# Expert 0's output for the last batch as seven products in token pairs, and earlier fetches of expert 1's weights

## The chip, the cores and the metric

The kernel runs on one core of one Trainium2 chip. The metric is the device time of one execution in microseconds (us); lower is better. Times called "at 115.84" are microseconds from the start of the profiled execution's span. The engines are called as the profile calls them: PE (TensorE; PEld is its weight load), DVE (VectorE), ACT (ScalarE), POOL (GpSimd) and SP (SyncE, here only a queue of transfers).

## What is computed

An attention over sorted blocks gives `x` (3072 tokens, 512 features); a mixture of eight experts, all of which see every token, is summed with routing weights `P`:

```python
# attention: 4 batches, 8 heads, 768 positions, 64 features; blocks sorted by a doubly normalised 8x8 matrix
x = attn_out.transpose(0, 2, 1, 3).reshape(3072, 512)
logits = x @ w_gate                       # 3072 x 8
P = np.exp(logits - logits.max())
for _ in range(8):                        # the routing's rounds
    P /= P.sum(1, keepdims=True) + 1e-09
    P /= P.sum(0, keepdims=True) + 1e-09
    P *= N / E
for e in range(E):                        # w1[e]: 512 x 1024, w2[e]: 1024 x 512
    h = np.maximum(x @ w1[e], 0.0)
    out += P[:, e:e + 1] * (h @ w2[e])
```

## The kernel before

**Stages.** Batch 0's attention comes first. Then the attention of batches 1 to 3 is woven with expert 0's work on batches 0 and 1 (`first_two`). From about 114.5 on, with the attention's buffers given back, expert 0 works on batches 2 and 3 (`last_two`, called `tail0` in the loop) while the routing's rounds run (`balance`, called `chain`). Behind that come experts 1 to 7, whose products all go by a seven-product scheme (Winograd's form of Strassen's: seven products of half size in place of eight, for sums and differences made beforehand).

**Expert 0.** `hidden0` makes `relu(x @ w1)` for 384 tokens: eight blocks `fb` of four 128x384 matmuls, each taken out of PSUM by ACT; one `next()` of it is one block. `output0` makes `h @ w2` for three tiles of 128 tokens: eight 128x512 matmuls each, and one `next()` is four of them. Batch 2's outputs are copied to `osbl` by ACT (`keep`); batch 3's are scaled with the routing weight `glog[:, t, 0]` on the way (`keep_scaled`). Copied tiles are scaled later, in SBUF, by ACT (`scale0`, 18 tiles).

**Experts 1 to 7.** `hidden(e, p, i, hT)` is one of four units for a third `p` of the tokens (1024): seven steps of two 128x512 matmuls, three ACT copies, one ACT relu and four DVE operations. `output7` is seven steps of four 128x256 matmuls for a pair of token tiles. `gather` adds a scaled product to `osbl` on DVE. Their operands are sums: `sum_w` (of w1), `sum_w2` (of w2) and `sum_h` (of the hidden layer) on POOL, `sum_x` (of x, line 139) on DVE. `sums(n)` issues the next n operations from the queue of POOL's sums.

**The rounds.** `balance` is a chain of small DVE operations (lines 446 to 475) on `glog`, 128x24x8, with small PE matmuls between them that sum over the partitions (lines 449, 454, 471). Each `yield` of it ends a piece; the loop of 56 steps says behind which step of `tail0` a piece goes. PE executes in the order in which the pinned matmuls are written, so a round's matmul that waits for DVE holds up what is written behind it. The pieces with matmuls stand behind steps 2, 4, and 8, 13, 17, 22, 26, 31, 35, 39. From step 28 on, one step of the first unit series of expert 1 (`first`, 28 steps) is written behind each step of `tail0`.

**Orders and queues.** `pin` puts an instruction behind whatever was written before it for its engine. Other instructions may be moved ahead by the scheduler that lays out each engine's stream before the run; `sum_x` on DVE, `scale0` on ACT and `balance`'s DVE operations are not pinned. Weights come by transfers issued on POOL (`load_w1`, line 81; `load_w2`, line 86), which share one queue with the loads of q, k and v (`load_batch`, line 72) and with half of the small transfers of sorted values (`vsb`, line 170; the other half goes by SP). Expert 1's w1 is fetched during batch 3's attention, w2 behind `sum_w(1)`. POOL's `sums(8)` stands at step 40 behind a one-operation gate (line 652) that reads `glog`, so that it starts when the rounds are over.

Of the kernel before, what the change touches and what calls it, by code (L numbers as in the profile page):

```python
# [13 lines left out]
F32 = mybir.dt.float32  # L14
BF16 = mybir.dt.bfloat16
AF = mybir.ActivationFunctionType
# [9 lines left out]
def kernel(  # L26
# [52 lines left out]
    def load_w1(e):  # L79
        w1t[e] = wp.tile([128, 4, F], BF16, name="w1e")  # L80
        pin(nc.gpsimd.dma_start(out=w1t[e],
                                in_=moe_w1[e].rearrange("(kk k) f -> k kk f", k=128)))

    def load_w2(e):
        w2t[e] = (wq if e else wcp).tile([128, 8, Dm], BF16, name="w2e")
        pin(nc.gpsimd.dma_start(out=w2t[e],
                                in_=moe_w2[e].rearrange("(fb k) f -> k fb f", k=128)))
# [222 lines left out]
    def output0(c0, hTs, obank, done):  # L310
        for tt in range(3):
            oacc = obank()
            for fb in range(8):
                pin(nc.tensor.matmul(oacc, hTs[:, fb, tt * 128:(tt + 1) * 128],
                                     w2t[0][:, fb, :], start=(fb == 0), stop=(fb == 7)))
                if fb == 3:
                    yield
            done(c0 // 128 + tt, oacc)
            yield

    def keep(t, oacc):
        (nc.vector.tensor_copy if t < 12 else nc.scalar.copy)(osbl[:, t, :], oacc)

    def keep_scaled(t, oacc):
        nc.scalar.activation(out=osbl[:, t, :], in_=oacc, func=AF.Copy,
                             scale=glog[:, t, 0:1])

    wct = {}

# [110 lines left out]
    def balance():  # L440
        onesc = mpc.tile([128, 128], F32)
        nc.vector.memset(onesc, 1.0)
        I128 = mpc.tile([128, 128], F32)
        nc.vector.tensor_copy(I128, Ibig)
        gm = mpc.tile([128, 1], F32)
        nc.vector.reduce_max(out=gm, in_=glog.rearrange("p t e -> p (t e)"), axis=AX.X)
        yield
        gmps = bank()[:, 0:128]
        pin(nc.tensor.matmul(gmps[0:1, :], gm, I128, start=True, stop=True))
        gm1 = mpc.tile([1, 1], F32)  # L450
        nc.vector.reduce_max(out=gm1, in_=gmps[0:1, :], axis=AX.X, negate=True)
        yield
        gnps = bank()[:, 0:128]
        pin(nc.tensor.matmul(gnps[:, 0:1], onesc[0:1, :], gm1, start=True, stop=True))
        gneg = mpc.tile([128, 1], F32)
        nc.vector.tensor_copy(gneg, gnps[:, 0:1])
        nc.scalar.activation(out=glog, in_=glog, func=AF.Exp, bias=gneg)

        rs2 = mpc.tile([128, NT], F32)
        cs2 = mpc.tile([128, E], F32)  # L460
        cs1 = mpc.tile([128, E], F32)
        yield
        for it in range(8):
            nc.vector.reduce_sum(out=rs2, in_=glog, axis=AX.X)
            nc.vector.tensor_scalar_add(rs2, rs2, 1e-9)
            nc.vector.reciprocal(out=rs2, in_=rs2)
            nc.vector.tensor_mul(glog, glog, mkap(rs2, [rs2.ap[0], rs2.ap[1], [0, E]]))
            nc.vector.reduce_sum(out=cs2, in_=glog.rearrange("p t e -> p e t"), axis=AX.X)
            yield
            csps = bank()[:, 0:128]  # L470
            pin(nc.tensor.matmul(csps[:, 0:E], onesc, cs2, start=True, stop=True))
# [3 lines left out]
            nc.vector.tensor_mul(glog, glog, mkap(cs1, [cs1.ap[0], [0, NT], cs1.ap[1]]))  # L475
            yield
# [141 lines left out]
    def sums(n):  # L618
        while n and queue:
            if next(queue[0], 0) is None:  # L620
                n -= 1
            else:
                queue.pop(0)

    def last_two():
        for bb, done in ((2, keep), (3, keep_scaled)):
            hT = htp.tile([128, 8, 1024], BF16, name="hT")
            halves = [(bb * S + c, hT[:, :, c:c + 384]) for c in (0, 384)]
            for c0, hTs in halves:
                yield from hidden0(c0, hTs, bank)  # L630
            for c0, hTs in halves:
                yield from output0(c0, hTs, lambda: op.tile([128, Dm], F32, name="oacc"), done)

    tail0, chain = last_two(), balance()
    x1, x2 = sum_x(1), sum_x(2)
    works = {0: x0, 10: x1, 14: x1, 19: x1, 23: x1, 41: x2, 43: x2, 46: x2, 48: x2}
    first = None
    for n in range(56):
        next(tail0)
        if n == 28:  # L640
            hT = htp.tile([128, 8, 1024], BF16, name="hT")
            first = units(1, 0, hT, pin)
        if first:
            next(first)
            if n == 28 + 21:
                sum_h(0, hT, 0, 3)
        if n in works:
            next(works[n], 0)
        if n in (0, 2, 4, 6, 8, 11, 13, 15, 17, 20, 22, 24, 26, 29, 31, 33, 35, 37, 39):
            next(chain)  # L650
        if n == 40:
            pin(nc.gpsimd.tensor_copy(held, glog[0:96, NT - 1, 0:2]))
            sums(8)

    hTs = {0: hT}

# [60 lines left out]
```

## Time and profile before

| What | Value |
|---|---|
| Time of three runs, median (lowest to highest) | 679.98 us (679.85 to 680.33) |
| The profiled execution: its own time; its span | 680.18 us; 678.2 us |
| Mean granted TensorE clock | 0.992 of full speed |
| Busy shares of the span: PE, DVE, POOL, ACT | 96%, 80%, 70%, 44% |
| Stage with `tail0`: start; first matmul of `output7` | 114.55; 172.51 |
| Rounds: first matmul (line 449); last `glog` update (line 475) | 116.59; 152.99 to 153.35 |
| `load_w1(1)` issued; `sum_w(1)`; `load_w2(1)` issued | 95.33; 104.14 to 113.25; 113.25 |

The span is what the profile shows of the engines; the execution's own time holds 1.98 us more around it. Busy shares are averages over stages with different limits.

### The profile page before, as it was taken

What the parts mean: (1) busy time and instruction counts of PE and PEld (TensorE: products, weight loads), DVE (VectorE), ACT (ScalarE), POOL (GpSimd) and SP (SyncE); (2) the same over time, 40 slices, a digit from 0 to 9 for tenths busy, and PEclk for the clock granted to TensorE, in tenths of its full rate; (3) what the DMA queues carried; (4) which work ended last, traced back from release to release, by engine and by line L of the source; (5) the groups of instructions that cost most, each with busy time, mean ns of one, the idle gap of its engine ahead of it and who ended that gap; (6) DMA issues with size and microseconds to landing.
All of it is one profiled execution on the core that took longest, in us unless ns stands there. A gap on an engine that the chain in (4) does not pass through costs nothing.

```text
span 678.2 us, 13166 instructions
## 1 busy us (share of the span) xinstructions
PE 651.5 (96%) x5033; PEld 436.5 (64%) x5108; DVE 545.2 (80%) x1154; ACT 298.5 (44%) x550; POOL 472.6 (70%) x499
## 2 busy tenths in 40 slices
PE   2999999999999999999999999999999999999996
PEld 1756766554566666666666666666666666666675
DVE  6727768763788888888988889888888889888896
ACT  3747764469533433334333343434333343333430
POOL 4542335007888988898997898689886999646745
PEclk9789999999999999999999999999999999999999
DMA  9898973100240330030303040034003120001223
GB/s 146 164 218 127 150 125 46 31 1 12 52 61 3 63 60 5 1 63 4 61 1 47 17 63 1 1 63 63 1 2 63 19 45 0 1 1 64 94 78 141
DMA packets 31903, 36.57 MB, mean 54 GB/s; under 512 B 2016, under 2 KB 24288, under 8 KB 31840
## 3 DMA queue, kind: packets, MB, share of 16 engines
q0 software_dynamic: 26400, 27.82, 25.9%
q1 hardware_dynamic: 5440, 7.90, 3.6%
q8 instruction: 40, 0.66, 0.4%
q14 instruction: 23, 0.19, 0.1%
HBM read 52.45 MB, written 6.29 MB: 87 GB/s over the span
## 4 chain that ended last, share of the span: by engine, by line
PE 72%; DVE 1%; issue 1%; POOL 1%; ACT 0%; DVEq 0%
PE oacc L574 37%; PE bk L487 34%; PE bk L574 1%; DVE osbl L539 1%; POOL hs L557 1%; DVE hT L523 0%; DVE hT L526 0%; ACT p L507 0%; DVEq L539 0%
## 5 line engine op out<-in xcount | busy, mean ns | idle before, releaser
L539 DVE SCALAR_TENSOR_TENSOR osbl<-oacc,glog,osbl 128x256 f32<-128x256 f32 (+1 forms) x490 | 255.7, 522 | 61.4 <-PE oacc L574 61.3
L557 POOL TENSOR_TENSOR hs<-hT 128x512 bf16<-128x512 bf16 (+2 forms) x105 | 99.5, 961 | 67.7 <-DVE hT L526 67.6
L487 PE MATMUL bk<-xtT,w1e 128*128 128x512 bf16 x475 | 143.5, 379 | 0.9
L574 PEld LDWEIGHTS <-hT 128*128 128x128 bf16 x1008 | 98.6, 98 | 64.5 <-issue 1.2
L574 PEld LDWEIGHTS <-hs 128*128 128x128 bf16 x1008 | 98.5, 98 | 64.5 <-POOL hs L557 1.5
L574 PE MATMUL oacc<-w2e,hT 128*128 128x256 bf16 x796 | 119.6, 273 | 1.0 <-ACT hT L529 0.5
L529 ACT ACTIVATE hT<-bk 128x512 bf16<-128x512 f32 x84 | 50.3, 599 | 158.2 <-PE bk L487 140.4
L557 POOL TENSOR_TENSOR hs<-hT,hs 128x512 bf16<-128x512 bf16 (+2 forms) x105 | 99.9, 959 | 4.9
L557 POOL TENSOR_TENSOR hs<-hs,hT 128x512 bf16<-128x512 bf16 (+2 forms) x105 | 100.0, 960 | 4.2 <-ACT hT L529 0.4
L487 PE MATMUL bk<-xc,wc 128*128 128x512 bf16 x319 | 96.3, 379 | 0.6 <-ACT p L507 0.2
L574 PE MATMUL oacc<-w2e,hs 128*128 128x256 bf16 x612 | 92.0, 273 | 1.6 <-POOL hs L557 0.9
L515 ACT COPY u<-bk 128x512 f32<-128x512 f32 x84 | 49.3, 587 | 95.4 <-PE bk L487 82.4
L487 PEld LDWEIGHTS <-w1e 128*128 128x128 bf16 x672 | 65.8, 98 | 10.4
L523 DVE CUSTOM_DVE_ANT_0 hT<-bk,p 128x512 bf16<-128x512 f32 x84 | 58.1, 692 | 11.5 <-ACT p L520 6.4
L533 DVE SCALAR_TENSOR_TENSOR h<-bk,hT 128x512 bf16<-128x512 f32 x84 | 57.2, 681 | 5.8 <-ACT hT L529 5.8
L520 ACT COPY p<-bk 128x512 f32<-128x512 f32 x84 | 49.4, 588 | 23.2 <-PE bk L487 23.2
L507 ACT COPY p<-bk 128x512 f32<-128x512 f32 x84 | 49.4, 588 | 20.3 <-PE bk L487 20.3
L511 DVE CUSTOM_DVE_ANT_0 hT<-bk,p 128x512 bf16<-128x512 f32 x84 | 57.3, 682 | 0.9 <-ACT hT L307 0.5
L526 DVE CUSTOM_DVE_ANT_0 hT<-bk,u 128x512 bf16<-128x512 f32 x84 | 57.2, 680 | 1.0 <-PE bk L487 1.0
L574 PE MATMUL oacc<-w2s,hs 128*128 128x256 bf16 x364 | 54.8, 273 | 0.3
L487 PEld LDWEIGHTS <-wc 128*128 128x128 bf16 x504 | 49.3, 98 | 8.0 <-issue 0.4
L487 PE MATMUL bk<-xc,w1e 128*128 128x512 bf16 x159 | 48.0, 379 | 0.0
(116 smaller groups left out, 834.9 us busy)
## 6 DMA issues: line engine op xcount, KB each, us to landing
w1e<-in_moe_w_dram POOLq DMA_DIRECT2D x8, 1024.0 KB, 8.2
w2e<-in_moe_w_dram POOLq DMA_DIRECT2D x8, 1024.0 KB, 8.9
out_dram<-osbl SPq DMA_DIRECT2D x23, 256.0 KB, 2.0
kvq<-in_v_dram POOLq DMA_DIRECT2D x3, 768.0 KB, 10.4
vsb<-vs SPq DMA_DIRECT2D x16, 97.5 KB, 4.3
vsb<-vs POOLq DMA_DIRECT2D x16, 97.5 KB, 3.9
kvq<-in_q_dram POOLq DMA_DIRECT2D x4, 384.0 KB, 12.9
kvq<-in_k_dram POOLq DMA_DIRECT2D x4, 384.0 KB, 13.5
```

Source lines behind the costliest of these rows:

```text
L487: hold(nc.tensor.matmul(ps, wa[:, kk, :], xa[:, kk, :], start=(first and kk == 0), stop=(kk == 1), skip_group_check=True))
L507: nc.scalar.copy(p1, u)
L511: nc.vector._custom_dve(TENSOR_ADD_SAT, out=c11, in0=w, in1=p1, s0=TOP, s1=0.0)
L515: nc.scalar.copy(u2, u)
L520: nc.scalar.copy(p5, v)
L523: nc.vector._custom_dve(TENSOR_ADD_SAT, out=c22, in0=u, in1=p5, s0=TOP, s1=0.0)
L526: nc.vector._custom_dve(TENSOR_ADD_SAT, out=c12, in0=v, in1=u2, s0=TOP, s1=0.0)
L529: nc.scalar.activation(out=c21, in_=u, func=AF.Relu)
L533: nc.vector.scalar_tensor_tensor(out=h3[e, p][:, i, :], in0=u, scalar=0.0, in1=c22, op0=ALU.max, op1=ALU.subtract)
L539: nc.vector.scalar_tensor_tensor(out=o, in0=ps, scalar=glog[:, t, e:e + 1], in1=o, op0=ALU.mult, op1=ALU.add)
L557: nc.gpsimd.tensor_tensor(out=c, in0=a, in1=b, op=o)
L574: nc.tensor.matmul(ps, h[:, fb, :], w[:, fb, :], start=(first and fb == 0), stop=(fb == 3), skip_group_check=True)
```

## The change

Three things. The 48 matmuls 128x512 of batch 3's outputs become, in three pairs of token tiles (18 and 21, 19 and 22, 20 and 23), 3 x 7 steps of four 128x256 matmuls; their w2 sums (`sum_w2_0`, eight POOL operations) and hidden sums (`sum_h0`, sixteen POOL operations, eight of them half as long) are new, and the outputs are taken out by four ACT operations and two DVE operations for each pair instead of two ACT operations. `load_w1(1)` moves from batch 3's attention to batch 2's. POOL's gate is gone: `sum_w2_0` and four operations of `sum_w2(1)` are written ahead of the loop, the other four at step 5 of `first`. The rounds all stand in the 44 steps ahead of the pairs (matmuls behind steps 2, 4, and 9, 15, 19, 23, 27, 33, 38, 43), and the 21 pair steps are written, three for every four, into the 28 steps of `first`. `w2s[0]` takes the first of the two buffers in which `load_w2(1)` was.

```diff
-    def hidden0(c0, hTs, hbank):
-        for fb in range(8):
+    def hidden0(c0, hTs, hbank, each=lambda n: None):
+        for n, fb in enumerate((0, 4, 1, 5, 2, 6, 3, 7)):
...
             nc.scalar.activation(out=hTs[:, fb, 0:384], in_=hps[:, 0:384], func=AF.Relu)
+            each(n)
             yield
...
                 load_batch(bb + 1, [(x, 0, 8) for x in "vkq"])
                 build_r(bb + 1, nc.gpsimd, 4)
+                if bb == 2:
+                    load_w1(1)
             else:
-                load_w1(1)
                 sums = sum_w(1)
...
-    load_w2(1)
...
+    hs0 = {}
+
+    w2s[0] = wq.tile([128, 4, 4, Dm // 2], BF16, name="w2e")
+    load_w2(1)
+
+    def sum_w2_0():
+        for k in (0, 2):
+            b11, b12 = (w2t[0][:, 4 + k:6 + k, d:d + 256] for d in (0, 256))
+            b21, b22 = (w2t[0][:, k:k + 2, d:d + 256] for d in (0, 256))
+            t1, t2, t3, t4 = (w2s[0][:, j, k:k + 2, :] for j in range(4))
+            for a, b, c in ((b12, b11, t1), (b22, t1, t2), (b22, b12, t3), (b21, t2, t4)):
+                pin(nc.gpsimd.tensor_tensor(out=c, in0=a, in1=b, op=ALU.subtract))
+
+    def sum_h0(i, hA, hB, f0=0, f1=4):
+        if f0 == 0:
+            hs0[i] = hsp.tile([128, 3, 4, 128], BF16, name="hs")
+        cs = slice(128 * i, 128 * i + 128)
+        s1, s2, s4 = (hs0[i][:, j, f0:f1] for j in range(3))
+        a11, a12 = hA[:, 4 + f0:4 + f1, cs], hA[:, f0:f1, cs]
+        a21, a22 = hB[:, 4 + f0:4 + f1, cs], hB[:, f0:f1, cs]
+        for a, b, o, c in ((a21, a22, ALU.add, s1), (s1, a11, ALU.subtract, s2),
+                           (a11, a21, ALU.subtract, a21), (a12, s2, ALU.subtract, s4)):
+            pin(nc.gpsimd.tensor_tensor(out=c, in0=a, in1=b, op=o))
+
+    def pair0(i, hA, hB):
+        a, b = 18 + i, 21 + i
...
+        def add(ps, h, w, first):
+            for fb in range(4):
+                pin(nc.tensor.matmul(ps, h[:, fb, :], w[:, fb, :], start=(first and fb == 0),
+                                     stop=(fb == 3), skip_group_check=True))
+
+        def put(t, c, ps):
+            nc.scalar.activation(out=osbl[:, t, c:c + 256], in_=ps, func=AF.Copy,
+                                 scale=glog[:, t, 0:1])
+
+        u, x = (op.tile([128, Dm], F32, name="oacc") for _ in range(2))
+        u, x0, x1 = u[:, 0:256], x[:, 0:256], x[:, 256:512]
+        add(u, hA[:, 4:8, cs], b11, True)
+        put(a, 0, u)
+        yield
+        add(x0, hA[:, 0:4, cs], b21, True)
+        yield
+        add(x1, s1, t1, True)
+        put(b, 256, x1)
+        yield
+        add(u, s2, t2, False)
+        put(a, 256, u)
+        yield
+        add(x1, s4, b22, False)
+        gather(0, a, 0, x)
+        yield
+        add(u, s3, t3, False)
+        gather(0, b, 256, u)
+        yield
+        add(u, hB[:, 0:4, cs], t4, False)
+        put(b, 0, u)
+        yield
+
+    def pairs0(hA, hB):
+        p = [pair0(i, hA, hB) for i in range(3)]
+        for i in (0, 0, 0, 0, 0, 1, 0, 1, 0, 1, 1, 1, 2, 1, 2, 1, 2, 2, 2, 2, 2):
+            next(p[i])
+            yield
+
     def last_two():
...
+        def each(n):
+            if n in (3, 7):
+                sum_h0(0, hA, hB, (n - 3) // 2, (n + 1) // 2)
+
+        yield from hidden0(3 * S, hA, bank)
+        yield from hidden0(3 * S + 384, hB, bank, each)
+        for i in (1, 2):
+            sum_h0(i, hA, hB)
+        yield from pairs0(hA, hB)
+
+    sum_w2_0()
+    sums(4)
     tail0, chain = last_two(), balance()
     x1, x2 = sum_x(1), sum_x(2)
-    works = {0: x0, 10: x1, 14: x1, 19: x1, 23: x1, 41: x2, 43: x2, 46: x2, 48: x2}
-    first = None
-    for n in range(56):
+    works = {0: x0, 11: x1, 17: x1, 21: x1, 25: x1, 47: x2, 51: x2, 55: x2, 59: x2}
+    rounds = (0, 2, 4, 6, 9, 10, 15, 16, 19, 20, 23, 24, 27, 28, 33, 34, 38, 39, 43)
+    for n in range(44):
         next(tail0)
-        if n == 28:
-            hT = htp.tile([128, 8, 1024], BF16, name="hT")
-            first = units(1, 0, hT, pin)
-        if first:
-            next(first)
-            if n == 28 + 21:
-                sum_h(0, hT, 0, 3)
...
-        if n in (0, 2, 4, 6, 8, 11, 13, 15, 17, 20, 22, 24, 26, 29, 31, 33, 35, 37, 39):
+        if n in rounds:
             next(chain)
-        if n == 40:
-            pin(nc.gpsimd.tensor_copy(held, glog[0:96, NT - 1, 0:2]))
-            sums(8)
+    hT = htp.tile([128, 8, 1024], BF16, name="hT")
+    first, n = units(1, 0, hT, pin), 0
+    for m in range(28):
+        next(first)
+        if m == 5:
+            sums(4)
+        if m == 20:
+            sum_h(0, hT, 0, 3)
+        while n * 28 < (m + 1) * 21:
+            next(tail0)
+            n += 1
...
```

More of the change, by code (lines that the diff above doesn't have):

```diff
@@ L322, in keep @@
         (nc.vector.tensor_copy if t < 12 else nc.scalar.copy)(osbl[:, t, :], oacc)
-    def keep_scaled(t, oacc):
-        nc.scalar.activation(out=osbl[:, t, :], in_=oacc, func=AF.Copy,
-                             scale=glog[:, t, 0:1])
     wct = {}
@@ L623, in sums @@
                 queue.pop(0)
-    def last_two():
-        for bb, done in ((2, keep), (3, keep_scaled)):
-            hT = htp.tile([128, 8, 1024], BF16, name="hT")
[L628 to L632, printed above, removed]
+    hs0 = {}
+    w2s[0] = wq.tile([128, 4, 4, Dm // 2], BF16, name="w2e")
@@ new lines, in pair0 @@
+    def pair0(i, hA, hB):
+        a, b = 18 + i, 21 + i
+        cs = slice(128 * i, 128 * i + 128)
+        s1, s2, s4 = (hs0[i][:, j] for j in range(3))
+        t1, t2, t3, t4 = (w2s[0][:, j] for j in range(4))
+        s3 = hB[:, 4:8, cs]
+        b11, b21, b22 = w2t[0][:, 4:8, 0:256], w2t[0][:, 0:4, 0:256], w2t[0][:, 0:4, 256:512]
+        def add(ps, h, w, first):
[27 more added lines that the diff above has]
+        yield
@@ new lines, in pairs0 @@
+    def pairs0(hA, hB):
[3 more added lines that the diff above has]
+            yield
+    def last_two():
+        obank = lambda: op.tile([128, Dm], F32, name="oacc")
+        hT = htp.tile([128, 8, 1024], BF16, name="hT")
+        for c in (0, 384):
+            yield from hidden0(2 * S + c, hT[:, :, c:c + 384], bank)
+        for c in (0, 384):
+            yield from output0(2 * S + c, hT[:, :, c:c + 384], obank, keep)
+        hT = htp.tile([128, 8, 1024], BF16, name="hT")
+        hA, hB = hT[:, :, 0:384], hT[:, :, 384:768]
+        def each(n):
[6 more added lines that the diff above has]
+        yield from pairs0(hA, hB)
@@ L634 @@
+    sum_w2_0()
+    sums(4)
     tail0, chain = last_two(), balance()
     x1, x2 = sum_x(1), sum_x(2)
-    works = {0: x0, 10: x1, 14: x1, 19: x1, 23: x1, 41: x2, 43: x2, 46: x2, 48: x2}
-    first = None
-    for n in range(56):
+    works = {0: x0, 11: x1, 17: x1, 21: x1, 25: x1, 47: x2, 51: x2, 55: x2, 59: x2}
+    rounds = (0, 2, 4, 6, 9, 10, 15, 16, 19, 20, 23, 24, 27, 28, 33, 34, 38, 39, 43)
+    for n in range(44):
         next(tail0)
-        if n == 28:
-            hT = htp.tile([128, 8, 1024], BF16, name="hT")
-            first = units(1, 0, hT, pin)
-        if first:
-            next(first)
-            if n == 28 + 21:
-                sum_h(0, hT, 0, 3)
@@ L647 @@
         if n in works:
             next(works[n], 0)
-        if n in (0, 2, 4, 6, 8, 11, 13, 15, 17, 20, 22, 24, 26, 29, 31, 33, 35, 37, 39):
+        if n in rounds:
             next(chain)
-        if n == 40:
-            pin(nc.gpsimd.tensor_copy(held, glog[0:96, NT - 1, 0:2]))
-            sums(8)
+    hT = htp.tile([128, 8, 1024], BF16, name="hT")
+    first, n = units(1, 0, hT, pin), 0
[8 more added lines that the diff above has]
+            n += 1
+            if 44 + n in works:
+                next(works[44 + n], 0)
```

## The prediction, made before the changed kernel ran

> **What bounds the kernel now.** I read the page first, then the timelines of PE, DVE, POOL and ACT from 95 to 185, then the table of stages, then single transfers.
>
> ```profile
> PE 651.5 (96%) x5033; PEld 436.5 (64%) x5108; DVE 545.2 (80%) x1154; ACT 298.5 (44%) x550; POOL 472.6 (70%) x499
> ...
> PE 72%; DVE 1%; issue 1%; POOL 1%; ACT 0%; DVEq 0%
> ```
>
> PE's matmuls are the path. In the table of stages every 40 us from 220 to 660 hold about 39.74 us of PE, so what PE gains or loses before 175 moves the end by as much. PE's losses there stand in the timeline of all engines at the start of the rounds:
>
> ```profile
> 115.84 1.28 DVE L139 TENSOR_TENSOR xc<-xtT 128x1024 bf16<-128x1024 bf16 x2
> ...
> 117.04 1.28 DVE L139 TENSOR_TENSOR xc<-xtT,xc 128x1024 bf16<-128x1024 bf16 x2
> ...
> 118.24 0.27 DVE L451 TENSOR_REDUCE gm<-bk 1x1 f32<-1x128 f32 x1
> ...
> 118.44 1.27 DVE L139 TENSOR_TENSOR xc<-xtT,xc 128x1024 bf16<-128x1024 bf16 x2
> ...
> 118.66 0.35 PE L454 MATMUL bk<-gm,onesc 1*128 1x1 f32 x2 [0.28 <-DVE gm L451]
> ...
> 119.64 0.14 DVE L456 COPY gneg<-bk 128x1 f32<-128x1 f32 x1
> ...
> 122.19 0.39 PE L471 MATMUL bk<-cs,onesc 128*128 128x8 f32 x2 [0.47 <-DVE cs L468]
> ```
>
> The scheduler has put six subtractions of `sum_x` (0.60 us start to start) into the first links of the rounds' chain: L451 and L456 leave DVE only behind them. By starts PE loses 0.45 us at L454 (eight hidden matmuls from 116.91 end their pitch of 0.1625 at 118.21), 0.65 at the first L471 (sixteen from 118.94: 121.54) and 0.44 at the third (eight 128x512 at 0.2158 from 127.11: 128.84; it starts at 129.28). POOL does nothing meanwhile:
>
> ```profile
> 113.25 0.94 POOL L86 DMA_DIRECT2D w2e<-in_moe_w_dram  x1
> 153.42 0.18 POOL L652 CAST held<-glog 96x2 bf16<-96x2 f32 x1 [39.24 <-DVE glog L475]
> ```
>
> At the seam to `output7` PE loses 1.03 us more (five groups reach 175.28 in place of 174.25), behind an ACT that is busy 19.10 of 19.10 us from 153.4 to 172.5.
>
> **The change part by part.** *The products.* 48 matmuls 128x512 at 0.2158 (twenty in 4.48 us, the last lasting 0.38) are 10.36 us; 84 of 128x256 at 0.1085 (a group of four and the next start 0.434 apart) are 9.11. Sum: −1.25 us, all of it on PE.
>
> *The rounds' places.* The least round from one L471 to the next is 3.05 us (133.81 until L468 ends at 136.79, and its start). A hidden step is 0.65 (138.40 to 139.04), an output step 0.863. The first L471 stands one hidden step later: the 0.65 goes. The next gaps are six hidden steps (3.9 us), four output steps (3.45, three times), six, five and five hidden steps (3.25 at least): all above 3.05. Only the third L471 may wait, by 0.1, because one subtraction (0.68) that must wait for batch 2's hidden steps falls into its round, as at 127.10. So 1.54 becomes 0.55: −1.0 us. The 0.45 at L454 stays.
>
> *POOL's new work ahead of the rounds.* Here a resource meets DVE that it did not meet before. The rows that show the meeting are the timeline at 61 and at 155, against a free one:
>
> ```profile
> 61.72 2.06 POOL L188 COPY qr<-kvq 128x768 bf16<-128x768 bf16 x2 [11.33 <-DMA kvq<-in_q_dram]
> 61.79 1.30 DVE L139 TENSOR_TENSOR xc<-xtT 128x1024 bf16<-128x1024 bf16 x1
> ...
> 85.60 0.68 DVE L139 TENSOR_TENSOR xtT<-xtT 128x1024 bf16<-128x1024 bf16 x1
> ...
> 155.61 0.89 DVE L139 TENSOR_TENSOR xtT<-xtT 128x1024 bf16<-128x1024 bf16 x1
> 155.91 1.61 POOL L437 TENSOR_TENSOR w2s<-w2e 128x512 bf16<-128x512 bf16 x1
> ```
>
> An L139 that starts inside a POOL operation takes 1.30 or 0.89 in place of 0.68, as long as that operation still lasts, and POOL's next operation waits for it in turn (1.61 for 1.15). The Trainium skill, SBUF — State Buffer, "SBUF: two separate sides", says it as a rule: the port pair that VectorE and GpSimd share is an exclusive lock for a whole instruction, taken by a VectorE operation with two SBUF inputs, and the other engine blocks fully; it speaks against POOL work at this place. By that rule the copy at L444 (SBUF to SBUF, one source, in a two-port mode) would wait as well, which no row here shows, and the sum would be some 0.3 us higher, an estimate.
>
> When is POOL busy? q of batch 3 lands at 74.4 + 14.3 = 88.7. w1 stands behind it in the queue and takes 5.8 more (w1 of expert 0 lands at 34.0, the w2 behind it at 39.8): 94.5. POOL's copies of batch 3 end at 95.4. `sum_w(1)` takes 9.1 (104.1 to 113.25): 104.5; the issue of w2 0.94: 105.5; `sum_w2_0` eight at 1.14: 114.6; w2 has landed by 104.5 + 9.0. `sums(4)`: 114.6 to 119.2 without a wait. The subtractions want 115.84 to 119.7. If the engines take turns, the four ahead of L451 run 116.9 to 117.5, behind POOL's next 118.65 to 119.25, 120.4 to 121.0, and 121.6: L451 is 3.4 us late, and L454, behind which PE's whole queue stands, with it. If DVE keeps the port once it has it, L451 is 1.1 late, L451 then lets POOL in, and L456 is 2.0 late. With POOL one microsecond later (a slower w1) it is 4.0; with the subtractions elsewhere it is 0. No row shows two DVE operations in a row against POOL. I take 3.4, since in both rows POOL's next operation comes right behind the DVE one. +3.4 us.
>
> *The pairs.* Each pair frees its accumulators by four `put`s and two gathers. A put is 0.4 to 0.55 us (a 512 copy 0.588, a 384 relu 0.490, scaling adds 0.13). `x1` must be free two pair steps after its put: 2.17 us (1.73 in the second pair), of which the group itself takes 0.60. ACT started 0.35 to 1.0 us behind PE in the saturated stretch, so some puts come 0 to 0.4 late. The last gather (0.48) has only 0.43 us of other matmuls in front of the step that waits for it: 0.3 to 1.0. Queued behind such a wait are PE's steps of `first`. Bounds 0 to 2.0; I take +0.6. A gain is excluded, since PE did not wait inside the old outputs (their groups follow at 1.30 us from 156.11 on). DVE's gathers (0.75 + 0.48, three times) lie beside 21 us in which it has some 4 us idle.
>
> *Hidden sums.* Sixteen POOL operations, 8 x 1.153 + 8 x 0.67 (between 0.43 for 128 and 0.92 for 384 columns) = 14.6 us, from the last hidden steps on. s1 of pair 1 is wanted about 9 us behind the last hidden step and is ready after 4.4; of pair 2, 16 against 9. Hidden; without that cover each operation late would cost 1.15. Their meeting with the last rounds' two-input operations (0.36) costs 0 to 0.5; I take 0.
>
> *w1 fetched sooner.* It needs no buffer back and 0.81 us of an idle POOL. But batch 3's sorted values (four on POOL's queue, issued 90.8 to 92.9; four on SP's) now meet it. Beside bulk loads, POOL's landed 0.3 to 1.7 us behind the last load and SP's took 6.7 in place of 3.3: 96 to 98.4 here, and they are wanted at 99.40. 0 to 1.0; I take +0.1.
>
> *The seam.* ACT still has 18 scales at 0.64, so I leave its 1.03.
>
> Sum: −1.25 − 1.0 + 3.4 + 0.6 + 0.1 = +1.85 on the profiled 680.18 (span 678.2 and 1.98 around it): 682.0. The median is 0.20 below the profiled run: 681.8.
>
> **Rivals.** *No meeting (faster).* The subtractions stand behind L451 and L456, or POOL is done before 115.8. Then the 3.4 goes: −1.55, 678.4 (677.7 to 680.0). For it: the scheduler lays the streams out anew. Against: by my clock POOL would have to be 3.4 us earlier, and the subtractions' data and buffers come free at the same moment as before. It decides as soon as POOL's last sum ends before 116.
>
> *Half a meeting (no change).* DVE keeps the port: 2.0 in place of 3.4, with pairs nearly free: 680.0 (679 to 681.3).
>
> *ACT becomes the bound (slower still).* From the last hidden step PE needs 28 x 0.433 + 21 x 0.434 = 21.2 us; ACT 16 x 0.48 + 12 x 0.5 + 18 x 0.64 = 25.2 if all scales are pulled in there. Before, the same count gave 22 for 19.1 us and PE lost 1.03, because scales are only put where the plan sees ACT idle. If the excess of 4 us lands on the puts, pairs cost 2.0 to 2.5 and the total is 683.5.
>
> *The fetch does not come sooner* because w1 holds up q instead of following it: then `queries` of batch 3 wait up to 5 us. Queue order in the rows speaks against it; it sits inside the slow cases.
>
> **How the numbers follow.** Forecast 0.36, no meeting 0.36, half a meeting 0.14, ACT-bound or fetch 0.14. About 0.2% (1.36 us) is what a measurement can tell. Faster by more: three quarters of the no-meeting case, 0.27. Slower by more: three quarters of the forecast (681.4 is near its lower half), the last case and little else, 0.43. The rest 0.30. Range: −2.25 with nothing lost gives 677.7; −2.25 + 4.0 + 2.0 + 0.1 gives 683.9. The forecast's own range is 680.4 to 683.9.
>
> **What would show it.** Right: L139 at about 117 to 123 with 1.2 to 1.8 us each and L437-like sums of 1.7 between them; PE idle 3 to 4 us before L454; L471 without waits later; 84 matmuls 128x256 into `oacc` at 0.1085 by 170. Wrong: L139 at 0.68 with POOL quiet, L454 at about 118.6; or PE idle inside the pairs of over 2 us; or a gap at 99 before the sorted values.

## The result, and the profile after

The changed kernel takes 683.64 us (median of six runs, 682.63 to 684.01) against 679.81 us for the kernel before (six runs, 679.26 to 680.33): ratio 1.0047, 95% interval 1.0037 to 1.0057. It is slower by 3.8 us; the forecast was 681.8, slower by 1.9. The profiled execution took 683.79 us, with a span of 682.0 and a mean granted clock of 0.986 (before: 680.18, 678.2 and 0.992).

Line numbers moved with the change. Before → after: the copy to `I` L444 → L440, the rounds' first reduction L451 → L447, the matmuls L449, L454, L471 → L445, L450, L467, POOL's sums of w2 L437 → L433, hidden matmuls of experts 1 to 7 L487 → L483, `output7` L574 → L570. The page's first line and the engine shares of its chain, after:

```profile
PE 653.2 (96%) x5069; PEld 440.8 (65%) x5144; DVE 543.8 (80%) x1160; ACT 299.6 (44%) x556; POOL 496.6 (73%) x522
...
PE 70%; DVE 2%; POOL 1%; ACT 1%; issue 1%; POOLq 0%; ACTq 0%; DVEq 0%
```

POOL has 24 us more work (472.6 before), and PE's share of the chain has gone from 72% to 70%, DVE's from 1% to 2%. Where, the timeline of all engines at the start of the rounds shows (start, duration, engine, line, operation; in brackets the idle time before it and who ended it):

```profile
114.01 1.16 POOL L433 TENSOR_TENSOR w2s<-w2e 128x512 bf16<-128x512 bf16 x1
114.94 0.30 DVE L440 CAST I<-Ibig 128x128 f32<-128x128 bf16 x1
...
115.43 3.08 DVE L139 TENSOR_TENSOR xc<-xtT 128x1024 bf16<-128x1024 bf16 x2
...
116.34 1.47 PE L305 MATMUL bk<-xtT,w1e 128*128 128x384 bf16 x8
116.35 1.60 POOL L433 TENSOR_TENSOR w2s<-w2e 128x512 bf16<-128x512 bf16 x1
...
117.92 1.60 POOL L433 TENSOR_TENSOR w2s<-w2e,w2s 128x512 bf16<-128x512 bf16 x1
118.43 2.24 DVE L139 TENSOR_TENSOR xc<-xtT,xc 128x1024 bf16<-128x1024 bf16 x2
120.59 0.27 DVE L447 TENSOR_REDUCE gm<-bk 1x1 f32<-1x128 f32 x1
...
121.00 0.55 PE L450 MATMUL bk<-gm,onesc 1*128 1x1 f32 x2 [3.19 <-DVE gm L447]
...
121.49 6.07 PE L305 MATMUL bk<-xtT,w1e 128*128 128x384 bf16 x20
...
127.40 0.28 PE L467 MATMUL bk<-cs,onesc 128*128 128x8 f32 x2
```

Two things stand here. First, the meeting: two L139 take 3.08 and 2.24 us where they took 1.28, POOL's sums between them 1.60 instead of 1.16, and L450 waits 3.19 us (0.28 before). Second, one that the prediction does not have: the twenty hidden matmuls behind L450 need 5.91 us from their first start to L467, where 20 x 0.1625 = 3.25. The table of windows (length; busy time and instructions of PE, PEld, DVE, ACT, POOL; then the granted TensorE clock, the DMA share, GB/s) says why:

```profile
118.40:120.20 1.80, 0.00 (x0) 0.00 (x0) 1.80 (x3) 0.00 (x0) 1.11 (x1) 0.97 0.00 0
120.20:121.00 0.80, 0.00 (x0) 0.03 (x1) 0.80 (x3) 0.00 (x0) 0.00 (x0) 0.50 0.00 0
121.00:124.00 3.00, 3.00 (x10) 1.66 (x11) 2.34 (x8) 0.95 (x2) 0.00 (x0) 0.50 0.00 0
124.00:126.80 2.80, 2.80 (x10) 1.36 (x9) 0.47 (x1) 0.98 (x2) 0.00 (x0) 0.50 0.03 6
126.80:130.00 3.20, 3.20 (x22) 1.99 (x21) 2.04 (x8) 2.28 (x5) 0.00 (x0) 0.98 0.00 0
```

While PE stood, its granted clock fell to half, and it stayed there until 126.9. The wait cost its own length, and then as much again.

Behind that, no L467 waits. The pairs (from 153.15 to the first `output7` group at 177.22) have PE wait again. PE's timeline there, the waits, and ACT's around the first:

```profile
156.85 0.59 PE L483 MATMUL bk<-xtT,w1e 128*128 128x512 bf16 x2 [0.50 <-ACT u L511]
161.23 0.59 PE L483 MATMUL bk<-xc,wc 128*128 128x512 bf16 x2 [0.32 <-ACT p L503]
```

```profile
154.63 0.47 ACT L659 ACTIVATE osbl<-oacc,glog 128x256 f32<-128x256 f32 x1 [0.26 <-PE bk L483]
155.00 1.32 ACT L605 ACTIVATE osbl<-osbl,glog 128x512 f32<-128x512 f32 x2
156.23 0.57 ACT L511 COPY u<-bk 128x512 f32<-128x512 f32 x1
```

Two scalings (L605, from `scale0`) have been laid in front of the copy L511 that frees a PSUM bank for PE. By starts, the pairs' groups come 1.96 us late in all: 0.67 and 0.49 at these two places, 0.11 to 0.25 at five more.

### The profile page after: what moved, and what is told of

The parts are those of the page before. It is cut to its first block, busy times and chain, and to the rows that moved or that the text cites. A ratio compares the mean times of both kernels' runs of the same rounds, so it can differ in the third digit from the quotient of the medians.

```text
span 682.0 us, 13286 instructions
## 1 busy us (share of the span) xinstructions
PE 653.2 (96%) x5069; PEld 440.8 (65%) x5144; DVE 543.8 (80%) x1160; ACT 299.6 (44%) x556; POOL 496.6 (73%) x522
## 4 chain that ended last, share of the span: by engine, by line
PE 70%; DVE 2%; POOL 1%; ACT 1%; issue 1%; POOLq 0%; ACTq 0%; DVEq 0%
PE oacc L570 35%; PE bk L483 34%; POOL hs L553 1%; DVE osbl L535 1%; PE oacc L655 1%; DVE h L529 1%; ACT hT L525 1%; DVE hT L519 0%; ACT osbl L605 0%; PE bk L570 0%; POOLq L794 0%; ACT u L511 0%; DVE hT L522 0%; ACT osbl L659 0%; ACT p L516 0%
## 5 line engine op out<-in xcount | busy, mean ns | idle before, releaser
L535 DVE SCALAR_TENSOR_TENSOR osbl<-oacc,glog,osbl 128x256 f32<-128x256 f32 (+1 forms) x496 | 251.9, 522 | 63.8 <-PE oacc L570 62.0
L483 PE MATMUL bk<-xtT,w1e 128*128 128x512 bf16 x475 | 155.0, 378 | 1.6 <-ACT u L511 0.5
L553 POOL TENSOR_TENSOR hs<-hT 128x512 bf16<-128x512 bf16 (+2 forms) x105 | 99.9, 961 | 62.4 <-DVE hT L522 62.3
L570 PEld LDWEIGHTS <-hT 128*128 128x128 bf16 x1008 | 98.6, 98 | 63.8 <-issue 1.2
L570 PEld LDWEIGHTS <-hs 128*128 128x128 bf16 x1008 | 98.0, 97 | 56.4 <-issue 0.8
L570 PE MATMUL oacc<-w2e,hT 128*128 128x256 bf16 x796 | 119.7, 273 | 0.4
L553 POOL TENSOR_TENSOR hs<-hs,hT 128x512 bf16<-128x512 bf16 (+2 forms) x105 | 100.2, 963 | 4.7
L553 POOL TENSOR_TENSOR hs<-hT,hs 128x512 bf16<-128x512 bf16 (+2 forms) x105 | 100.0, 961 | 4.9
L483 PE MATMUL bk<-xc,wc 128*128 128x512 bf16 x318 | 96.0, 379 | 0.8 <-ACT p L503 0.3
L570 PE MATMUL oacc<-w2e,hs 128*128 128x256 bf16 x612 | 91.7, 272 | 0.7
L511 ACT COPY u<-bk 128x512 f32<-128x512 f32 x84 | 49.4, 588 | 95.4 <-PE bk L483 85.8
L483 PEld LDWEIGHTS <-w1e 128*128 128x128 bf16 x672 | 65.8, 98 | 18.5 <-issue 1.6
L570 PE MATMUL oacc<-w2s,hs 128*128 128x256 bf16 x364 | 54.5, 272 | 0.3
L483 PEld LDWEIGHTS <-wc 128*128 128x128 bf16 x504 | 49.3, 98 | 7.0 <-issue 0.7
L483 PE MATMUL bk<-xc,w1e 128*128 128x512 bf16 x159 | 48.0, 379 | 0.1
```

What stands on the lines that cost most here:

```text
L483: hold(nc.tensor.matmul(ps, wa[:, kk, :], xa[:, kk, :], start=(first and kk == 0), stop=(kk == 1), skip_group_check=True))
L511: nc.scalar.copy(u2, u)
L553: nc.gpsimd.tensor_tensor(out=c, in0=a, in1=b, op=o)
L570: nc.tensor.matmul(ps, h[:, fb, :], w[:, fb, :], start=(first and fb == 0), stop=(fb == 3), skip_group_check=True)
```

## The account

Each row is one profiled execution, in us from the span's start, and differences. "Start" is the first matmul of the rounds (L445, before L449); "stand" is from there to L450, with 8 x 0.1625 of matmuls and some 0.4 of its own in it; "next" from L450 to the first L467 (one hidden step, 0.65, shorter in the kernels with the old places of the rounds); "total" from the start to the last group of matmuls of the kernel. The kernels below the first two are the experiments that follow.

| Kernel | Start | Stand | Next | Total |
|---|---|---|---|---|
| before | 116.59 | 2.07 | 3.53 (0.47 of it wait) | 557.41 |
| after | 116.03 | 4.97 | 6.40 | 561.84 |
| after, subtractions held (a_sumx) | 116.84 | 1.71 | 3.57 | 555.21 |
| after, 18 fillers (a_fill) | 116.85 | 4.96 | 3.62 | 559.12 |
| after, scalings held (a_scale) | 116.61 | 4.96 | 5.22 | 560.11 |
| after, four sums later (a_sums_gate) | 117.73 | 2.07 | 3.62 | 557.52 |
| a_sumx without the products (a_noprod) | 116.88 | 1.71 | 3.94 | 556.54 |
| both held (a_both) | 116.84 | 1.72 | 3.57 | 555.02 |
| before, subtractions held (b_sumx) | 116.40 | 1.71 | 3.07 | 556.10 |

The starts differ between executions by what comes early in them: the first L192 is already at 70.46 before and at 69.89 after, the same 0.57 apart, and over all traces here it lies between 69.82 and 71.85. From one fixed matmul of batch 3's attention (L192 near 98.4) to the start, before, after and the first held kernel need the same: 98.42 to 116.59, 97.86 to 116.03 and 98.67 to 116.84 are 18.17 each. So the earlier fetch of w1 shows no cost and no gain at PE.

After against before the total is +4.43: the stand +2.90; the half clock 6.40 − 3.57 = +2.83; the products −1.25, worked out and not measured here; the waits of the first and third round gone, −1.09; the pairs +1.96; the seam to `output7` −0.62 (its third group starts 2.15 behind the first, 2.77 before); the last output's wait for POOL's L553 0.88 to 0.2, −0.7. Sum +4.03; 0.4 are not placed.

## The experiments

The theory: POOL's sums and VectorE's subtractions share something that only one of them holds at a time; the subtractions, laid into the first link of the rounds by the scheduler, are stretched; PE stands; the stand brings the clock down. The rivals: VectorE's order alone, without POOL; ACT in the pairs; products that cost as much as they save.

**The subtractions held in their written place.** `sum_x(1)` and `sum_x(2)` then stand behind the rounds' pieces, and POOL's sums meet none of them.

```diff
 def sum_x(p):
...
-            nc.vector.tensor_tensor(out=c, in0=a, in1=b, op=ALU.subtract)
+            (pin if p else lambda ins: ins)(nc.vector.tensor_tensor(out=c, in0=a, in1=b, op=ALU.subtract))
```

> The changed kernel, with sum_x(1) and sum_x(2) kept in the written order on DVE, so that their six first subtractions stand at steps 11, 17, 21 of the rounds and later, when POOL is idle, and not ahead of the chain's links at L447 and L452. PE, ACT and POOL streams are the same as in the changed kernel. Theory 1 (the subtractions meet POOL's last four w2 sums, PE stands for 3.4 us at L450, and its clock then halves for 20 matmuls, 2.7 us): both go, L450 starts at about 117.7, the 20 matmuls behind it take 3.3 us, the subtractions last 0.68 us, and the kernel takes 677.6 us (677.0 to 678.6). Rival A (PE waits there for something else, the sums' memory traffic or the order of the rounds): 683.6, unchanged. Rival B (the clock drop is set by the clock's own window and not by the wait): about 3 us gained, 680.5.

Measured: 678.09 us (677.57 to 679.08), ratio to before 0.9964, interval 0.9950 to 0.9977, inside the range written: 5.5 us faster than the change, and faster than the kernel before. The timeline of all engines at the same place:

```profile
116.04 1.15 POOL L433 TENSOR_TENSOR w2s<-w2e,w2s 128x512 bf16<-128x512 bf16 x1
...
117.14 1.15 POOL L433 TENSOR_TENSOR w2s<-w2e 128x512 bf16<-128x512 bf16 x1
117.25 0.28 DVE L447 TENSOR_REDUCE gm<-bk 1x1 f32<-1x128 f32 x1 [0.95 <-PE bk L445]
118.26 1.15 POOL L433 TENSOR_TENSOR w2s<-w2e,w2s 128x512 bf16<-128x512 bf16 x1
118.55 0.29 PEld L450 LDWEIGHTS bk<-gm,onesc 1*128 1x128 f32 x2 [0.32 <-ACT hT L307]
118.55 0.38 PE L450 MATMUL bk<-gm,onesc 1*128 1x1 f32 x2
```

POOL's sums last 1.15 each, the reduction waits for PE rather than PE for it, and the clock is 1.00 from 114 on. Stand and half clock are both gone.

**Fillers in the stand.** Is the half clock a cost of its own? The wait is left and PE is kept busy in it.

```diff
+        if n == 4:
+            fill = bank()
+            for _ in range(18):
+                pin(nc.tensor.matmul(fill[:, 0:384], w1t[0][:, 0, 0:128], xtT[:, 0, 0:384],
+                                     start=True, stop=True))
         if n in rounds:
             next(chain)
```

> The changed kernel, with 18 more matmuls (128x384 into a bank that nobody reads) written ahead of L450, so that PE works through 2.9 of the 3.36 us that it stands there. Nothing else moves. Theory 1 (the clock falls because PE stands): L450 still starts at about 121.0 and the subtractions still last 1.1 to 1.6 us each, but the granted clock stays at 1.00 and the 20 matmuls behind take 3.3 in place of 5.9 us: 680.9 us (680.3 to 681.6). Rival (the 20 matmuls are slow for another reason, such as late operands or contention): 683.6, or later by what the extra matmuls add.

Measured: 681.84 us (681.17 to 683.15), ratio 1.0018 (1.0009 to 1.0026). The subtractions take 3.07 and 2.24 as before, and L450 comes 4.96 behind the start, yet:

```profile
118.40:121.80 3.40, 3.16 (x20) 1.69 (x19) 3.40 (x5) 0.60 (x2) 1.92 (x2) 1.00 0.00 0
121.80:125.40 3.60, 3.59 (x22) 2.15 (x22) 2.83 (x8) 2.19 (x5) 0.00 (x0) 1.00 0.00 0
```

In its windows the clock stays at 1.00, and the next 20 matmuls need 3.62 with L450 instead of 6.40. Idle matmuls made the kernel 2 us faster; the profiled totals differ by 2.72. The time came out 0.9 above the 680.9 written and above its range (680.3 to 681.6). That forecast took the whole 2.7 of the profiled execution for every execution of the change; the last runs below suggest that the clock's fall is not the same in each, but other executions were not traced.

**The scalings held.** `scale0`'s 18 operations keep their written place on ACT, one `output7` group ahead of their use.

```diff
-            nc.scalar.activation(out=osbl[:, t, :], in_=osbl[:, t, :], func=AF.Copy,
-                                 scale=glog[:, t, 0:1])
+            pin(nc.scalar.activation(out=osbl[:, t, :], in_=osbl[:, t, :], func=AF.Copy,
+                                     scale=glog[:, t, 0:1]))
...
         if m == 20:
             sum_h(0, hT, 0, 3)
+            scale0((0, 4))
...
-                scale0([t for t in (8 * p + i, 8 * p + 4 + i) if t < 18])
+                j = 4 * p + i + 1
+                scale0([t for t in (8 * (j // 4) + j % 4, 8 * (j // 4) + 4 + j % 4) if t < 18])
```

> The changed kernel, with scale0's eighteen ACT operations kept in the written order and written one output7 unit ahead of their use, so that only two of them stand inside the pairs. Theory 2 (inside the pairs PE loses 2.0 us behind ACT, where 18 scales stand between the copies that PE waits for): the stretch from the first pair step to output7 shrinks from 24.1 to 22.1 to 22.6 us, the waits of L483 on L511 and L503 vanish, and the kernel takes 681.8 us (681.3 to 682.3). Rival (the pairs lose it on the accumulators' own handover by puts and gathers, so that ACT's load does not matter): 683.3 to 683.8. If the scales are missed later, experts' outputs wait for them and the time is over 684.

Measured: 684.26 us (682.70 to 684.80), ratio 1.0050 (1.0036 to 1.0064): a miss. The mechanism is as thought, the price not. No L483 waits for ACT any more and the pairs lose 1.02 us instead of 1.96. But from the last L467 on the kernel needs 524.31 us against 524.86, 0.55 less, because part comes back at the end. PE's timeline of this kernel, and the same place in the change:

```profile
665.71 0.28 PE L570 MATMUL oacc<-w2e,hs 128*128 128x256 bf16 x1 [0.88 <-POOL hs L553]
```

```profile
667.94 0.60 PE L570 MATMUL oacc<-w2e,hs 128*128 128x256 bf16 x4
```

Of what PE gains in the pairs, 0.88 stands again as a wait for POOL's last hidden sums, which the kernel before had too. So the ACT rival explains about half of the waits in the pairs (0.94 of 1.96) and hardly any of the time. Four of the six runs took 684.2 to 684.8 with a mean clock of 0.984, against 682.70 and 0.988 in the profiled execution; that the clock's fall was longer in them fits, but is not shown.

**POOL's sums ahead of the rounds, in the kernel before.** This part of the change alone: w1 fetched in batch 2's attention, the gate taken away, `sums(8)` ahead of the loop; products and rounds as before.

```diff
                 build_r(bb + 1, nc.gpsimd, 4)
+                if bb == 2:
+                    load_w1(1)
             else:
-                load_w1(1)
...
+    sums(8)
     tail0, chain = last_two(), balance()
...
-        if n == 40:
-            pin(nc.gpsimd.tensor_copy(held, glog[0:96, NT - 1, 0:2]))
-            sums(8)
```

> The kernel before, with only POOL's share of the change: w1 of expert 1 fetched in batch 2's attention, the gate gone and the eight sums of its w2 written ahead of the rounds; no seven products. Theory 1: the sums run from about 113.5 to over 122, the six subtractions meet them, L451 comes 3 to 4 us late, PE's clock halves behind it, and the next links (L467 and L475 have two inputs in SBUF too) wait as well: 685 us (683.5 to 686.5). Rival A (the meeting costs only together with the moved rounds or the pairs): 679.8 or less. Rival C (the waits come but the clock does not fall): 682.5 to 683.5.

Measured: 686.24 us (685.37 to 689.03), ratio 1.0088 (1.0071 to 1.0105): as expected. Eight sums run through the meeting instead of four. Timelines of DVE and PE:

```profile
118.49 3.19 DVE L139 TENSOR_TENSOR xc<-xtT,xc 128x1024 bf16<-128x1024 bf16 x2
```

```profile
122.02 0.35 PE L455 MATMUL bk<-gm,onesc 1*128 1x1 f32 x2 [3.85 <-DVE gm L452]
122.30 4.46 PE L305 MATMUL bk<-xtT,w1e 128*128 128x384 bf16 x16
```

Sixteen matmuls take 4.46 where 2.76 is their full-clock time in the same trace. One part of the change, put on the kernel before, does more harm than the whole.

**The cure from POOL's side.** VectorE's order is left as the scheduler made it; four sums move to where batch 2's first output is kept.

```diff
     sum_w2_0()
-    sums(4)
...
+        if n == 18:
+            pin(nc.gpsimd.tensor_copy(held, osbl[0:96, 12, 0:2]))
+            sums(4)
         if n in rounds:
             next(chain)
```

> The changed kernel with one thing moved: POOL's first four sums of w2(1) (L433, 1.16 to 1.60 us each, beside L139 at 114 to 119.5) start only when the first output tile of batch 2 is kept, near 134 us, behind a small copy by POOL that waits for it. VectorE's order is as the scheduler made it (four L139 ahead of the reduction that the rounds wait for). If the meeting of POOL's sums and VectorE's subtractions is the cause, two L139 take 1.3 us instead of 3.08 and 2.24, the L450 matmul waits some 0.9 us (115.4 + 4 x 0.64 + 0.5 = 118.5 against 117.6), the granted clock stays at 1.00, and the time is 678.8 (678.2 to 679.8). Rival, the order on VectorE alone is the cause, whatever POOL does: the wait stays near 3 us, 682 or more. Rival, any meeting of POOL's sums with VectorE costs this much: the rounds at 134 to 139 then wait for 2 us, 680.8.

Measured: 680.19 us (679.69 to 682.08), ratio 1.0001 (0.9992 to 1.0010), between my value (678.8, at most 679.8) and the second rival's (680.8), and nearer to the latter. The first meeting is gone: two L139 take 1.28 and 1.29, L450 waits 0.28, the clock stays at 1.00. VectorE's order alone therefore is not the cause. But the sums met the rounds instead (timeline of DVE, POOL and PE):

```profile
131.62 1.15 POOL L433 TENSOR_TENSOR w2s<-w2e,w2s 128x512 bf16<-128x512 bf16 x1
...
131.88 1.10 DVE L471 TENSOR_TENSOR glog<-glog,cs 128x192 f32<-128x192 f32 x1
132.73 1.26 POOL L433 TENSOR_TENSOR w2s<-w2e 128x512 bf16<-128x512 bf16 x1
133.02 0.35 DVE L460 TENSOR_REDUCE rs<-glog 128x24 f32<-128x192 f32 x1
133.41 0.62 DVE L461 TENSOR_SCALAR rs<-rs 128x24 f32<-128x24 f32 x1
133.96 1.15 POOL L433 TENSOR_TENSOR w2s<-w2e,w2s 128x512 bf16<-128x512 bf16 x1
...
134.40 0.92 DVE L463 TENSOR_TENSOR glog<-glog,rs 128x192 f32<-128x192 f32 x1
...
135.91 0.39 PE L467 MATMUL bk<-cs,onesc 128*128 128x8 f32 x2 [1.03 <-DVE cs L464]
```

L471 takes 1.10 and L463 0.92 in place of 0.36, L461 0.62 in place of 0.18, and the reduction L460 its 0.35 as ever: an operation with two SBUF inputs waits for POOL's current sum to end, the scaling with one input (L461) too, a reduction not, and the reciprocal L462 not either (0.30 at 134.06, as without a sum). The round is late by 1.03 at L467.

**The products taken out of the held kernel.** Batch 3's output as before, without its sums; the subtractions held. The output's 12 steps are spread over the same 28 steps of `first`. The second `sums(4)`, still at step 5 of `first`, has none of the hidden sums ahead of it on POOL any more.

```diff
...
-        yield from hidden0(3 * S + 384, hB, bank, each)
-        for i in (1, 2):
-            sum_h0(i, hA, hB)
-        yield from pairs0(hA, hB)
+        yield from hidden0(3 * S + 384, hB, bank)
+        for c, h in ((0, hA), (384, hB)):
+            yield from output0(3 * S + c, h, obank, keep_scaled)
...
-    sum_w2_0()
     sums(4)
...
```

> The changed kernel with sum_x(1) and sum_x(2) held in their written place (as in the run that took 678.09 us), but the last batch's output of expert 0 computed as before: six products of eight 128x512 matmuls, no sums of w2(0) (L632) and of hidden values (L643), 12 steps spread over the same 28. Work on TensorE: 48 x 0.2165 = 10.39 us instead of 84 x 0.1085 = 9.11, so +1.28. Against it stand the waits that the pairs bring, 1.59 us in that run between the last round and the first group of output7, which should go, while the wait of the first output7 group for the hidden values, 0.68 + 0.36 in the profile of before, should come back. Mine: 678.8 (678.0 to 679.5), the products gain little because their waits eat it. Rival A, the saved matmuls are a gain in full: 679.4 or more. Rival B, the products cost more than they save: under 678.1.

Measured: 679.60 us (679.18 to 680.96), ratio 0.9986 (0.9977 to 0.9995). Against 0.9964 with the products that is 1.5 us more, by the totals 1.33. The time is rival A's, but not all of it belongs to the products. POOL's eight sums of w2(1) now run in one go, from 114.69 to 123.98, and the last of them meet the rounds (timeline of DVE and PE):

```profile
120.81 1.04 DVE L463 TENSOR_TENSOR glog<-glog,rs 128x192 f32<-128x192 f32 x1
...
122.53 0.36 PE L467 MATMUL bk<-cs,onesc 128*128 128x8 f32 x2 [0.21 <-DVE cs L464]
```

From the start to the last L467 this kernel needs 0.44 us more than the held one (31.34 against 30.90), nearly all of it at this wait; from there to the end it needs 0.89 more, which is the products' with all that they change behind them. That lies between my 0.7 and rival A's 1.3, so this run does not decide between the two. The old outputs wait nearly as much as the pairs: between the last L467 and `output7` PE loses 1.30 us by starts here, and 1.57 in the held kernel.

**Both held.** The edits of the first and third run together.

> The changed kernel with sum_x held in its place and scale0's 18 scalings held one output7 group ahead of their use, instead of wherever ScalarE had room among the pairs. The pairs' waits fall from 1.59 to 1.02 us and the two groups behind them gain some 0.4 (both as the trace of the run with the scalings alone showed), but that run gave 0.7 back at the end, where the last output waits 0.9 us for POOL's sums L553. Mine: 677.8 (677.2 to 678.4), against 678.09 without the scalings held. Rival, the whole loss in the pairs is ScalarE's: 676.5. Rival, holding the scalings costs: 678.5 or more. The median of the run with the scalings alone was 684.26 while its profiled execution took 682.70 with the granted clock low for a shorter stretch (5.2 us from L450 to the first L467, 6.4 in the profile of the change); if the clock's fall is what spread those runs, the runs here, without a fall, lie within 1.5 us.

Measured: 677.87 us (677.21 to 678.30), ratio 0.9959 (0.9945 to 0.9972). The fastest here, but by 0.2 us over the first run (677.57 to 679.08), which these spreads don't tell apart. No L483 waits in the pairs any more, and the 0.88 at L553 is back.

**The subtractions held in the kernel before.** The control.

```diff
-    works = {0: x0, 10: x1, 14: x1, 19: x1, 23: x1, 41: x2, 43: x2, 46: x2, 48: x2}
+    works = {0: x0, 12: x1, 16: x1, 21: x1, 25: x1, 41: x2, 43: x2, 46: x2, 48: x2}
```

(and the line of `sum_x` as in the first run)

> Control: the kernel before with sum_x(1) and sum_x(2) held in their written place, sum_x(1) two steps later than before so that it starts behind the first round. No POOL sums run there. The waits of L454 (0.28), the first L471 (0.47) and the third (0.27) may go. Mine: 679.7 (679.0 to 680.6): the edit that made the changed kernel 5.5 us faster is worth under 1 us here, since nothing meets; the rest of the 2.4 us by which the mended change beats before is then the change's own. Rival, holding the subtractions is worth 2.4 us by itself: 678.1.

Measured: 679.07 us (678.70 to 680.84), ratio 0.9981 (0.9973 to 0.9990). The three waits of the rounds vanish (the total falls by 1.31), which is more than the "under 1 us" written, with the time inside its range. The edit that took 5.5 us from the change takes 1.3 from the kernel before; the change, mended, is ahead of it by 0.9981 − 0.9964, 1.2 us.

**How long must PE stand?** The filler kernel with 6 and with 3 matmuls in place of 18.

> The changed kernel with 6 of the 18 filler matmuls (128x384, 0.1625 us each) in front of L450, whose results nothing uses: TensorE then stands 3.2 - 6 x 0.1625 = 2.2 us instead of 3.2. How long must the stand be for the clock to fall? If a stand of 2.2 us is too short, the granted clock stays at 1.00 through 114 to 130 and the time is that of the run with 18 fillers, 681.8 (681.0 to 682.6). Rival, a stand of this length brings it down as well: the clock shows 0.50 to 0.60 for several us behind L450 and the time is 683.6.

> As the run with 6, with 3 filler matmuls: TensorE stands 3.2 - 3 x 0.1625 = 2.7 us. If the fall needs about 3.2 us, the clock stays at 1.00 and the time is 681.8 (681.0 to 682.6); if 2.7 us suffice in some executions, the times spread from 681.5 to 684 and the mean granted clock goes down with the slow ones; if in all, 683.6.

Measured: 682.47 us with 6 (680.82 to 684.55), 683.02 us with 3 (681.17 to 684.56). The medians rise with the stand, but the runs lie far apart:

| PE stands before L450 | Runs, us |
|---|---|
| 0.25 (18 fillers) | 12 between 681.2 and 683.2 |
| 2.20 (6) | 5 between 680.8 and 681.9; 5 between 683.1 and 684.6 |
| 2.69 (3) | 4 between 681.2 and 682.1; 6 between 682.9 and 684.6 |
| 3.19 (none, the change) | 6 between 682.6 and 684.0 |

The profiled execution with 6 took 681.01 and shows a clock of 1.00 behind the stand; the one with 3 took 684.56 and shows a fall. Windows at both ends of the fall, of the change, of the kernel with the scalings held, and of that with 3 fillers:

```profile
120.00:120.40 0.40, 0.00 (x0) 0.00 (x0) 0.40 (x2) 0.00 (x0) 0.00 (x0) 0.59 0.00 0
...
126.80:127.20 0.40, 0.40 (x3) 0.20 (x2) 0.00 (x0) 0.38 (x1) 0.00 (x0) 0.87 0.00 0
```

```profile
122.00:122.40 0.40, 0.40 (x3) 0.25 (x2) 0.40 (x2) 0.00 (x0) 0.00 (x0) 0.70 0.00 0
...
125.20:125.60 0.40, 0.40 (x3) 0.19 (x2) 0.00 (x0) 0.00 (x0) 0.00 (x0) 0.54 0.00 0
```

```profile
123.80:124.20 0.40, 0.40 (x4) 0.18 (x3) 0.27 (x2) 0.10 (x1) 0.00 (x0) 0.69 0.00 0
...
127.00:127.40 0.40, 0.40 (x3) 0.21 (x2) 0.00 (x0) 0.11 (x1) 0.00 (x0) 0.55 0.00 0
```

A slice at 0.59 was at half for 0.82 of its 0.40 us. So the first fall lasts from 120.07 to 126.90, the second from 122.16 to 125.57, the third from 123.95 to 127.36: 6.83, 3.41 and 3.41 us. It comes in pieces of 3.41, and begins anywhere from 0.9 us before PE resumes to 1.0 after. The cost follows: 2.8 us with two pieces, 1.6 with one (a_scale's "next" of 5.22), none where the fall does not come. In the 3.41 us ahead of each of these falls PE was idle for 2.3 to 2.8. With 6 fillers, only 1.7 us of idle time fell into one such stretch (119.24 to 122.65, counted on in steps of 3.413 from that execution's fall at 27.09), and the clock stayed. That fits a clock that is set anew every 3.41 us by what the last stretch held, at a phase of its own in each execution: in the change the clock is also at half from 24.50 to 34.74, and 120.07 lies 28 x 3.413 us behind 24.50. Idle time is not all that counts, since in the 3.41 us ahead of 24.50 PE was idle for 0.96 only.

That the other runs of each kernel are split by this fall is not shown, since only one execution of each was traced. With 6 fillers the mean clocks of the shorter and the longer runs overlap (0.988 to 0.997 and 0.983 to 0.990). And executions differ ahead of the rounds too: of the 3.55 us between the two profiled executions with 6 and with 3 fillers, 2.03 are there by the first L192 (69.82 and 71.85), and 1.52 come behind the start. So whether a stand of 2.20 us can bring the clock down stays open.

## Why the prediction was right, and where it was not

The direction was right; the sum was 2 us short (+1.85 written, +3.8 measured), by the steps that follow. That 683.64 still lies in the forecast's 680.4 to 683.9 is in part luck: its upper bound (which adds up to 683.8) is made of a meeting of 4.0, pairs of 2.0 and a fetch of 0.1, and the time came near it with a meeting of 2.9, pairs of 1.96 and a cost of the clock that no bound holds. The rival that makes ACT the bound comes nearest, with 683.5, and for a reason that the run with the scalings held does not bear out.

- *The meeting.* Forecast +3.4 at L454 (2.0 to 4.0); measured +2.90. The mechanism is as it was written, turns included: L139, sum, L139, sum. The forecast had L139 at 1.2 to 1.8 each between sums of 1.7; they took 3.08 and 2.24 for two, and 1.60. The fourth subtraction ran free at 0.68, because the last sum had ended by then; so the meeting cost less than forecast. POOL was not 3.4 us early: its sums ran from 114.01 to 119.5, forecast 114.6 to 119.2. Two runs show the cause from both sides, the subtractions moved and the sums moved. The Trainium skill, SBUF — State Buffer, "SBUF: two separate sides", has the rule of the exclusive lock; the traces agree, also on the copy that no row of before showed: L440 took 0.30 beside a sum and 0.16 without.
- *The step that failed: that PE, late by so much, would lose so much.* The sum priced the stand at its own length. The clock's fall behind it, +2.83 in the profiled execution, is missing, and no rival has it. The Trainium skill, TensorE: Matmul & The Clock Gate, "Part 1: The HAM clock gate", tells of half rate after an idle window of some 3.4 us that runs freely; the length of the falls here, 3.41 and 6.83, agrees. The page asks for a whole idle window; here 2.3 to 2.8 idle us in 3.41 came ahead of the three falls shown, the least of the stands being 2.69.
- *The pairs.* Forecast +0.6 (0 to 2.0); measured +1.96 by starts. The term was mis-sized: it priced the puts' own lateness and not the scalings laid in front of the copies. That case stood among the rivals with 2.0 to 2.5, and with the wrong consequence: without those scalings the kernel gains 0.55 or less, because the last output gives part of it back. And not all the waits are the pairs' own: the old outputs at the same place lose 1.30 where the pairs lose 1.57.
- *The products.* Forecast −1.25, waits apart; net of the waits on both sides, −0.89 from the last L467 to the end, by the traces of the kernels with and without them. The −1.33 by the totals holds 0.44 of another meeting.
- *The rounds' places.* Forecast −1.0; −1.09. No L467 waits.
- *The seam.* Left at 1.03, measured 0.4: −0.6, probably since scalings were spent in the pairs. *The fetch.* Forecast +0.1 (0 to 1.0); 0.00 by three traces. *The hidden sums.* Taken as hidden; L139 at 152.89 took 0.90 beside them, without a wait of PE.
- *"No meeting", 678.4.* Given 0.36 as what the scheduler might do; done by hand it took 678.09.

## What to carry to other kernels

Before work goes to POOL, look what VectorE does at that moment and whether a wait of the path hangs on it; an instruction that the scheduler may move belongs pinned where two engines would meet. A stall of TensorE of 2.7 us or more was here not paid at its length alone: look at the granted clock behind it, and keep the engine busy with something, even with matmuls that nobody reads, where the stall can't be taken away. A wait that vanishes inside a stage is a gain only when the kernel's last wait does not grow by as much. Taking work off an engine lets what stood behind it start sooner, so a run without a part can meet something new and price that along with the part.

## What the runs showed of the hardware

The clock fell to 0.50 in pieces of 3.41 us at stands of 2.7 to 3.9 us, and one such piece cost some 1.6 us. An operation on 24 columns (L461) took 0.62 us in place of 0.18 beside a POOL sum, while reductions kept their 0.35 (L460, with the four sums later) and 0.50 (L464 at 121.89, without the products). A bf16 subtraction of 128x1024 and a POOL sum of 128x512, queued against each other, took turns at some 1.6 us each, in place of 0.68 and 1.15.
